# Column tiles, 32-row scores, zero products and turns of heads in an attention-plus-SSM kernel

## The chip, the cores and the metric

The kernel runs on one core of a Trainium2 chip. The metric is the device time of the core in microseconds (us), the median of several executions. The engines are TensorE (PE in the profile; PEld is its weight loads), VectorE (DVE), ScalarE (ACT), GpSimd (POOL) and SyncE (SP). ns is nanoseconds.

## The reference

Two independent halves are joined along the last axis. Half A is a complex diagonal state-space model (SSM), half B attention with 32 query heads of 20 columns and one key/value head, both over 2048 positions of 640 columns in bf16.

```python
def _A_ref(x, ...):                       # cut
    Bu = jnp.einsum("bld,pd->blp", x + 0j, B_bar)
    for t in range(L):
        h = Lam_bar[None, :] * h + Bu[:, t, :]
    # ... stacked to hseq
    y = 2.0 * jnp.einsum("blp,dp->bld", hseq, Cmat).real + x * Dskip
def _B_ref(x, wq, wk, wv, wo):            # S=2048, D=640, H=32, Dh=20
    scores = jnp.einsum("bhqd,bkd->bhqk", q, k) * (Dh ** -0.5)
    p = _softmax(scores, axis=-1)
    o = jnp.einsum("bhqk,bkd->bhqd", p, v)
    # ... heads joined, @ wo
```

## The kernel before

The work is cut into 2048 score tiles of 128 keys by 512 queries, in 32 blocks of four heads. Each tile needs one score product, an exponential, and one or more products with V (PV below) that add into one PSUM bank per block.

- A score product uses 21 rows of the array (20 head columns and a bound that keeps the exponential in range). Four heads lie at partitions 0, 32, 64 and 96, so up to four score products run side by side in row tiles (four start at 302.92 us in the timeline below).
- The exponential of most tiles is done by ScalarE, in groups of three and two tiles (tiles SC to PR). The others go to VectorE (tiles MB to DR), which builds the bits of four shifted bf16 values; their sum is the exponential. Such a tile costs four VectorE instructions and four PV products.
- A PV product has 32 output columns, so four heads run side by side in column tiles (four start within 10 ns at 302.37 us below).
- Everything else (projections, the SSM, the normalization, the output products) is "background", on the whole 128x128 array.

The static order on every engine comes from a planner in the kernel itself: it steps through a model of the engines, in which each operation has a duration, and picks the ready operation of the best priority.

```python
class Schedule:
    OUT = {"pe": 200.0, "act": 130.0, "dve": 110.0, "pool": 150.0, "dma": 60.0}
    OWN = {"pe": 0.0, "act": 60.0, "dve": 55.0, "pool": 100.0}
    # ... no cost for a change of the array's shape
class Build:
    CHUNKS = (3, 2)   # score tiles per ScalarE instruction
    MISC = 2          # PSUM banks shared by background and VectorE's tiles
    NPS = 5
    NDS = 4
    SHARE = 0.215
    # ...
    def mm(self, out, lhsT, rhs, start, stop, **kw):
        return lambda e: e.matmul(out, lhsT=lhsT, rhs=rhs, start=start, stop=stop, **kw)
    def score(self, op, m, out, bank):
        # ...
        op.fns.append(self.mm(out, p.KT[32 * j:32 * j + 21, 128 * kc:128 * kc + 128],
                              p.QT[32 * j:32 * j + 21, qb % 2, gg, :], True, True, tile_position=(32 * j, 0)))
    def pv(self, op, b, group):
        # ...
            op.fns.append(self.mm(bank.tensor[32 * j:32 * j + 32, bank.off:bank.off + 512], lhs, rhs,
                                  first, last, tile_position=(0, 32 * j), skip_group_check=True))
```

Of the kernel before, what the change touches and what calls it, by code (L numbers as in the profile page):

```python
# [20 lines left out]
class Op:  # L21
# [3 lines left out]
                 "seq", "land", "dma_key", "idx", "tail")  # L25

    def __init__(self, eng, fns, dur, deps=(), prio=5, reads=(), writes=(), prev=None, gate=None, hook=None,
                 dma_key=None, land=0.0, tail=0.0):
        self.eng, self.fns, self.dur = eng, list(fns), dur
        self.deps, self.prio, self.prev = list(deps), prio, prev  # L30
        self.reads, self.writes = list(reads), list(writes)
        self.gate, self.hook = gate, hook
        self.dma_key, self.land, self.tail = dma_key, land, tail
        self.start = self.end = None
        self.seq = self.idx = 0


class Schedule:
# [7 lines left out]
    OWN = {"pe": 0.0, "act": 60.0, "dve": 55.0, "pool": 100.0}  # L46
    URGENT = 1.0

    def __init__(self):
        self.t = 0.0  # L50
        self.pending = {e: [] for e in self.ENGINES}
        self.free = {e: 0.0 for e in self.ENGINES}
        self.order = []
        self.events = []
        self.procs = []
        self.dma_free = {}
        self.n = 0
        self.sources = {e: [] for e in self.ENGINES}
        self.slack = {"pe": 60.0, "dve": 150.0}

# [40 lines left out]
    def begin(self, op, eng):  # L101
        if op.hook is not None:
            op.hook(op)
        op.start = self.t
        if op.dma_key is not None:
# [9 lines left out]
        for lag in (0.0, 55.0, 60.0, 100.0, 110.0, 130.0, 150.0, 200.0):  # L115
            self.at(op.end + lag)

    def pick(self, eng):
        best = None
# [3 lines left out]
        for src in self.sources[eng]:  # L123
            extra = src()
            if extra is not None:
                cands = cands + [extra]
        for op in cands:
# [5 lines left out]
            if r <= t + 1e-6:  # L133
                if best is None or (op.prio, op.seq) < (best.prio, best.seq):
                    best = op
            elif op.prio <= self.URGENT and (urgent is None or r < urgent):
                urgent = r
        if best is None:
            return None
        if urgent is not None and best.prio > self.URGENT and t + best.dur > urgent + self.slack.get(eng, 1e9):  # L140
            return None
# [203 lines left out]
class Build:  # L345
    CHUNKS = (3, 2)
    MISC = 2
    NPS = 5
    NDS = 4
    SHARE = 0.215  # L350

    SHIFTS = ((0, 0.24037683), (32, 0.20213201), (64, 0.16997209), (96, 0.14292892))

# [49 lines left out]
    def alloc(self, o):  # L403
# [9 lines left out]
        self.QT = sb(o, "QT", [128, 2, NGG, 512], BF16)  # L413
# [3 lines left out]
        self.DR = sb(o, "DR", [128, self.NDS, len(self.SHIFTS), 512], I16)  # L417
        self.WO4 = sb(o, "WO4", [128, NGG, 640], BF16)
        self.PR = sb(o, "PR", [128, self.NPS, 3, 512], BF16)
# [13 lines left out]
        self.lift = sb(o, "lift", [128, 2], FP32)  # L433
# [20 lines left out]
    def alloc_late(self, s):  # L454
        self.W = self.sb(s, "W", [128, NC, 2, 512], BF16)
        self.g = self.sb(s, "g", [128, 2, 2, 512], BF16)
        self.OT = self.sb(s, "OT", [128, 12, 512], BF16)
        self.LATE = [f"W{c}" for c in range(NC)] + [f"g{u}_{i}" for u in range(2) for i in range(2)] \
            + [f"OT{i}" for i in range(12)]


    def pe(self, fns, dur, **kw):
        return self.s.add("pe", fns, dur, **kw)
# [28 lines left out]

    def mm(self, out, lhsT, rhs, start, stop, **kw):
        return lambda e: e.matmul(out, lhsT=lhsT, rhs=rhs, start=start, stop=stop, **kw)  # L494

    @staticmethod
    def mmt(n, k=1):
        return n / 2.3 * 1.0 + 8.0 * k
# [10 lines left out]
    def program(self):  # L509
# [5 lines left out]
        self.evac_op, self.norm_op = {}, {}  # L515
# [7 lines left out]
        self.d_per = {}  # L523
# [16 lines left out]
        self.s.sources["pe"].append(self.d_source)  # L540

    def warm_source(self):

        if self.started or self.s.t > 40000.0:
# [3 lines left out]
                  deps=[self.zero_op], reads=["PR0"], writes=[self.pvbank.key], hook=self.warm_last)  # L548
# [4 lines left out]
    def constants(self):  # L553
# [19 lines left out]
        many("VP", [lambda e: e.memset(p.VP[:], 0.0), lambda e: e.memset(p.VP[:, :, 20:21], 1.0)], 500)  # L573
# [3 lines left out]
        for k, (_, c) in enumerate(self.SHIFTS):  # L577
            fns.append(lambda e, k=k: e.memset(p.VS[:, k, :, 20:21], hi[k]))
            fns.append(lambda e, k=k, c=c: e.memset(p.VS[:, k, :, 21:22], c - hi[k]))
        many("VS", fns, 250)  # L580
        many("maskM", [
# [22 lines left out]
                                               channel_multiplier=1)], 250)  # L604
        rows = self.dve(lambda e: e.tensor_reduce(out=p.lift[:, 0:1], in_=p.E1[:], axis=AX.X, op=ALU.add), 120,
# [147 lines left out]
    def qt_task(self, qb, gg, bank):  # L753
        p = self
        prev = None
        slot = qb % 2
        for c in range(NC):
# [3 lines left out]
                           prio=3, reads=[f"xbT{qb}", "wq4"], writes=[bank.key])  # L761
        dst = p.QT[:, slot, gg, :]
        key = f"QT{slot}_{gg}"
# [11 lines left out]
        if qb == 0 and gg == 0:  # L775
            for c in range(NC):
# [7 lines left out]
                          deps=[m, self.lift_op], reads=[bank.key, "lift"], writes=[key, "QTr0_0"], prio=0.4)  # L784
# [14 lines left out]
    def row_task(self, qb, half, bank):  # L799
        p = self  # L800
        slot = qb % 2
# [3 lines left out]
        fns = [self.mm(bank.tensor[0:32, bank.off:bank.off + 512], p.Mm[:, gg, :], p.aq[:, gg % 4, :], gg == ggs[0],  # L805
                       gg == ggs[-1]) for gg in ggs]
        prev = self.pe(fns, 4 * self.mmt(512), deps=[self.mm_op] + [self.qt_op[(qb, gg)][1] for gg in ggs] + bank.last,
                       prio=1.5, reads=["Mm"] + [f"aq{i}" for i in range(4)], writes=[bank.key])
# [4 lines left out]
        if qb == 0 and half == 0:  # L813
            lo, ng = 1, 3
        fns = [lambda e, j=j: e.dma_start(p.QT[32 * j + 20:32 * j + 21, slot, lo:lo + ng, :],
# [3 lines left out]
                                           reads=[f"brow{rs}"] + [f"QT{slot}_{gg}" for gg in range(lo, lo + ng)],  # L819
                                           writes=[f"QTr{slot}_{gg}" for gg in range(lo, lo + ng)], prio=0, land=500.0)  # L820
# [13 lines left out]
    def attention(self):  # L834
# [10 lines left out]
        while self.tile_n < NTILE:  # L845
# [14 lines left out]
            fill = self.pe([], self.mmt(512, 2), deps=deps, prio=0, hook=lambda op, i=i: self.fill(op, i))  # L860
            self.next_fill = fill
            k += 1

    def fill(self, op, i):
# [7 lines left out]
        extra = None  # L872
        if self.want_d():
            tiles.append(self.tile_n)
            self.tile_n += 1
            extra = min(tiles, key=lambda m: self.d_per.get((m // 64, m % 4), 0))
            tiles.remove(extra)
# [4 lines left out]
        if extra is not None:  # L882
            self.fill_d(op, extra)
        op.reads = sorted(set(op.reads))
        op.dur = self.mmt(512, len(op.fns))
        dst = p.PR[:, h.index, 0:n, :]
        ex = self.act(lambda e: e.activation(dst, t[:, 0:512 * n], ACT.Exp, scale=1.0 / UNIT), 0.833 * 512 * n + 93,  # L887
# [12 lines left out]
    def score(self, op, m, out, bank):  # L900
# [5 lines left out]
        op.fns.append(self.mm(out, p.KT[32 * j:32 * j + 21, 128 * kc:128 * kc + 128],  # L906
                              p.QT[32 * j:32 * j + 21, qb % 2, gg, :], True, True, tile_position=(32 * j, 0)))
        op.reads += [f"KT{kc // 4}", f"QT{qb % 2}_{gg}", f"QTr{qb % 2}_{gg}"]
# [3 lines left out]
    def want_d(self):  # L912
        s = self.s
        if self.tile_n >= NTILE - 8 or self.d_count + 1 > self.SHARE * (self.tile_n - 16):
            return False
        if self.d_bank() is None:
            return False
        h = self.dhold[self.ndhold % self.NDS]
        return not h.taken or (h.left == 0 and s.done(h.users))

    def d_source(self):

        f = self.next_fill
        if f is None or f.start is None and f.deps and self.d_count == 0:
            return None
        if f.start is None:
            r = self.s.ready(f)
            if r is not None and r < self.s.t + self.ALONE:
                return None
        b = self.tile_n // 64  # L930
        if not self.started or not self.want_d() or not self.block_ready(b):
# [5 lines left out]
        def hook(op):  # L937
            self.tile_n += 1
            self.fill_d(op, self.tile_n - 1)
            op.reads = sorted(set(op.reads))  # L940
        return Op("pe", [], self.mmt(512, 1), prio=0.95, hook=hook)

    next_fill = None
    ALONE = 450.0

    def d_bank(self):
        s = self.s
        for b in self.free_banks:
            if all(o.end is not None and s.seen(o, "pe") <= s.t for o in b.last):
                return b  # L950
        return None
# [6 lines left out]
    def fill_d(self, op, m):  # L958

        p = self  # L960
        bank = self.d_bank()
# [4 lines left out]
        self.d_per[(m // 64, m % 4)] = self.d_per.get((m // 64, m % 4), 0) + 1  # L966
# [4 lines left out]
        first = self.dve(self.ts(p.DR[:, h.index, 0, :], bank.ap, 16256.0, 0.0, ALU.add, ALU.max), 600, deps=[op],  # L971
                         reads=[bank.key], writes=[k0], prio=0.5)
        self.s.spawn(self.d_give(bank, first))
        for k, (sh, _) in enumerate(self.SHIFTS):
            key = f"DR{h.index}_{k}"
            o = first
            if k:
                o = self.dve(self.ts(p.DR[:, h.index, k, :], p.DR[:, h.index, 0, :], float(sh), None, ALU.add), 200,
                             deps=[first], reads=[k0], writes=[key], prio=0.55)
# [3 lines left out]
    def pv_source(self):  # L983
# [23 lines left out]
        prio = 0.9 if tight else 2.0  # L1007
        return Op("pe", [], self.mmt(512, len(group)), prio=prio, hook=lambda op: self.pv(op, b, group))
# [5 lines left out]
    def pv(self, op, b, group):  # L1014
        p = self
        bank = self.pvbank
        for j, e in group:
            lhs, kc, rhs, key, ex, h, vk = e
# [20 lines left out]
    def norm_task(self, b, bank):  # L1039
# [3 lines left out]
        ot = b % 12  # L1043
        m1 = self.pe([self.mm(bank.cols(4 * i, 4 * i + 4), src[:, 128 * i:128 * i + 128], p.E1[:], True, True)
                      for i in range(4)], 4 * 65, deps=[self.evac_op[b], self.c_op["E1"]] + bank.last, prio=1.6,
                     reads=[f"pvsb{slot}", "E1"], writes=[bank.key])

        def rc(e):
            with p.nc.allow_low_precision("bf16 reciprocal of softmax denominator"):
                return e.reciprocal(p.rdT[:, slot, :], bank.cols(0, 16))  # L1050
        r = self.dve(rc, 230, deps=[m1], reads=[bank.key], writes=[f"rdT{slot}"], prio=1.2)
        spread = bass.AP(tensor=p.rdT, offset=16 * slot, ap=[[32, 128], [1, 16], [0, 32]])
        x = self.pool(lambda e: e.tensor_copy(p.rdX[:, slot, :, :], spread), 700, deps=[r], reads=[f"rdT{slot}"],  # L1053
                      writes=[f"rdX{slot}"], prio=1)
        fns = [self.mm(bank.cols(128 * i, 128 * i + 128),
                       p.rdX[:, slot, 4 * i:4 * i + 4, :].rearrange("p j d -> p (j d)"), p.ident[:], True, True)
               for i in range(4)]
        m2 = self.pe(fns, 4 * 65, deps=[x, self.c_op["ident"]], prio=1.6, reads=[f"rdX{slot}", "ident"],
                     writes=[bank.key])
        d = self.dve(self.tt(p.OT[:, ot, :], src, bank.ap, ALU.mult), 630, deps=[m2],  # L1060
# [406 lines left out]
```

## Time and profile before

985.23 us median of 3 runs (984.86 to 987.18); the profiled execution took 980.32. Lines of the page of before: busy us and share of each engine; busy tenths in 40 slices of the span; PEclk, the granted TensorE clock in tenths; and the shares of the chain of waits that ended last.

```profile
PE 908.5 (93%) x6555; PEld 262.0 (27%) x6555; DVE 741.0 (76%) x1899; ACT 813.4 (83%) x699; POOL 32.2 (3%) x66
...
ACT  3597789988777999977979999899798979688992
...
PEclk8987679966557999976969999799697868689987
...
PE 65%; DVE 19%; ACT 11%; issue 3%; DMA 1%; ACTq 0%; POOL 0%; POOLq 0%; DVEq 0%
...
L494 PE MATMUL SC<-QT,KT 21*128 21x512 bf16 x1711 | 303.7, 439 | 36.7 <-ACT PR L887 20.9
L506 DVE TENSOR_SCALAR DR<-MB 128x512 int16<-128x512 f32 x337 | 230.8, 687 | 121.7 <-PE MB L494 110.7
```

TensorE is the busiest engine and has most of the chain. ScalarE, which has the exponentials, has holes all along. The last two lines give the split: 1711 score tiles go to ScalarE and 337 to VectorE.

A busy share of TensorE can deceive, as matmuls overlap (below, each takes 0.39 to 0.61 us while the next group starts 0.32 to 0.54 us after it). The start times are surer. Timeline of TensorE in before, two short stretches (start us, us, engine, line, what, shapes, count):

```profile
302.37 0.61 PE L494 MATMUL MB<-DR,VS 128*32 128x512 bf16 x1
302.38 0.61 PE L494 MATMUL MB<-PR,VP 128*32 128x512 bf16 x1
302.38 0.61 PE L494 MATMUL MB<-DR,VS 128*32 128x512 bf16 x2
302.92 0.60 PE L494 MATMUL MB<-QT,KT 21*128 21x512 bf16 x1
302.92 0.61 PE L494 MATMUL SC<-QT,KT 21*128 21x512 bf16 x3
...
308.35 0.39 PE L494 MATMUL SC<-QT,KT 21*128 21x512 bf16 x2
308.67 0.39 PE L494 MATMUL MB<-PR,VP 128*32 128x512 bf16 x1
308.67 0.39 PE L494 MATMUL MB<-DR,VS 128*32 128x512 bf16 x1
308.68 0.39 PE L494 MATMUL MB<-PR,VP 128*32 128x512 bf16 x2
309.00 0.60 PE L494 MATMUL MB<-xbT,wq 128*128 128x512 bf16 x2
```

Four PV products start within 10 ns and count as one group. In the second stretch a group starts 0.32 to 0.33 us after one of another shape, and two of the same shape can start 0.216 us apart. In the first stretch the same step takes 0.54 us; there the clock's record stands at 0.5 (until 307.4 us, then at 1.0). Over all 512-column groups after 45 us, with the clock records laid beside them: same shape (PV after PV, whole array after whole array) at least 215 ns, median 225 to 226, at full clock, and at least 398, median 401 to 405, at half; change of shape, medians of 312 to 332 and 535 to 567. By these figures a change cost about 100 ns at full clock (312 less 215 is 97) and about 140 at half.

In the record of before the clock is either 1.0 or 0.5, in steps of 3.4 us (its periods are multiples of 3.413 us). After the start (from about 41 us on, to the end of the clock's record) it stands at half for 318 us in 24 periods, one of them 61 us long.

### The profile page before, as it was taken

Reading aid. Unit: us, or ns where it says so; the run is one execution under the profiler, and the core shown is the slowest. Engines: PE = TensorE matmul, PEld = TensorE weight load, DVE = VectorE, ACT = ScalarE, POOL = GpSimd, SP = SyncE. Lnnn points to the kernel's source line nnn. Section 1 sums busy time; section 2 is a strip of 40 time slices with the busy share of each in tenths; the row PEclk is TensorE's granted clock in tenths of the full one; section 3 lists DMA queues with packets and bytes.
Section 4 is the critical chain, followed back from the end, with each engine's and each line's share of the span. In section 5 each row is a group of like instructions: output and inputs, shape, how many; then the busy total and the mean of one; then the engine's idle time right before and its main releaser. Section 6 shows DMA issues by size and latency. Waiting matters only on the chain.

```text
span 978.6 us, 16125 instructions
## 1 busy us (share of the span) xinstructions
PE 908.5 (93%) x6555; PEld 262.0 (27%) x6555; DVE 741.0 (76%) x1899; ACT 813.4 (83%) x699; POOL 32.2 (3%) x66
## 2 busy tenths in 40 slices
PE   7889999999899999999899999989999999998997
PEld 2322222222123322222233322222332322223323
DVE  6987678978775588876956797799576868688672
ACT  3597789988777999977979999899798979688992
POOL 4000000000000000000000000000000000000000
PEclk8987679966557999976969999799697868689987
DMA  9740000000000010000000100000000000000000
GB/s 164 118 87 1 1 2 1 1 1 2 2 1 6 23 38 12 7 1 1 2 6 17 34 11 8 11 1 1 5 14 12 1 11 6 6 6 1 17 12 27
DMA packets 49147, 16.63 MB, mean 17 GB/s; under 512 B 43572, under 2 KB 49072, under 8 KB 49072
## 3 DMA queue, kind: packets, MB, share of 16 engines
q1 hardware_dynamic: 44480, 14.72, 7.1%
q10 hardware_dynamic: 4592, 0.88, 0.7%
q8 instruction: 52, 0.85, 0.4%
q14 instruction: 23, 0.19, 0.1%
HBM read 1.69 MB, written 5.24 MB: 7 GB/s over the span
## 4 chain that ended last, share of the span: by engine, by line
PE 65%; DVE 19%; ACT 11%; issue 3%; DMA 1%; ACTq 0%; POOL 0%; POOLq 0%; DVEq 0%
PE MB L494 47%; PE SC L494 18%; ACT PR L887 11%; DVE DR L506 7%; DVE DR L505 6%; DVE prod L501 1%; DMA vec<-in_A_Dskip_dram 1%; DVE pvsb L1032 1%; DVE stg L1098 1%; DVE u L501 0%; DVE g L1255 0%; DVE W L501 0%; DVE fr L506 0%; DVE QT L769 0%; ACTq L485 0%
## 5 line engine op out<-in xcount | busy, mean ns | idle before, releaser
L887 ACT ACTIVATE PR<-SC 128x1536 bf16<-128x1536 f32 (+1 forms) x685 | 802.2, 1244 | 124.9 <-PE SC L494 71.8
L494 PE MATMUL MB<-PR,VP 128*32 128x512 bf16 x1711 | 339.5, 448 | 4.4 <-DVE pvsb L1032 1.9
L494 PE MATMUL SC<-QT,KT 21*128 21x512 bf16 x1711 | 303.7, 439 | 36.7 <-ACT PR L887 20.9
L506 DVE TENSOR_SCALAR DR<-MB 128x512 int16<-128x512 f32 x337 | 230.8, 687 | 121.7 <-PE MB L494 110.7
L494 PE MATMUL MB<-DR,VS 128*32 128x512 bf16 x1348 | 311.2, 465 | 1.9 <-DVE pvsb L1032 1.6
L505 DVE TENSOR_SCALAR DR<-DR 128x512 int16<-128x512 int16 x1011 | 233.5, 288 | 9.8
L494 PE MATMUL MB<-QT,KT 21*128 21x512 bf16 x337 | 147.6, 439 | 7.3 <-DVE DR L506 4.4
L494 PEld LDWEIGHTS SC<-QT,KT 21*128 21x128 bf16 x1711 | 67.3, 93 | 291.8 <-issue 132.1
L494 PEld LDWEIGHTS MB<-PR,VP 128*32 128x32 bf16 x1711 | 73.0, 97 | 120.5 <-issue 95.6
L494 PEld LDWEIGHTS MB<-DR,VS 128*32 128x32 bf16 x1348 | 66.2, 100 | 74.3 <-issue 55.7
L494 PE MATMUL MB<-xaT,BT 128*128 128x512 bf16 x200 | 73.2, 440 | 1.6 <-DVE DR L506 1.6
L494 PE MATMUL MB<-CT,W 128*128 128x128 bf16 (+1 forms) x320 | 63.0, 313 | 0.0
L494 PE MATMUL MB<-xbT,wq 128*128 128x512 bf16 x165 | 54.8, 424 | 1.3 <-DVE QT L769 1.1
L494 PE MATMUL MB<-WO,OT 128*128 128x128 bf16 (+1 forms) x256 | 53.1, 346 | 0.7 <-DVE DR L506 0.5
L501 DVE TENSOR_TENSOR prod<-MB,Z 128x1024 bf16<-128x1024 f32 x40 | 48.4, 1211 | 6.5 <-PE MB L494 6.4
L1053 POOL COPY rdX<-rdT 128x512 bf16<-128x512 bf16 x32 | 22.3, 698 | 916.7 <-DVE rdT L1050 916.7
L1098 DVE CAST stg<-MB 128x512 bf16<-128x512 f32 x40 | 27.4, 684 | 30.9 <-PE MB L494 30.8
L494 PEld LDWEIGHTS MB<-QT,KT 21*128 21x128 bf16 x337 | 31.2, 93 | 49.3 <-DVE DR L506 20.5
L1255 DVE TENSOR_TENSOR_SCAN g<-sc,hst,u 128x512 bf16<-128x512 f32 x30 | 38.2, 1285 | 0.0
L501 DVE TENSOR_TENSOR OT<-pvsb,MB 128x512 bf16<-128x512 bf16 x32 | 21.8, 682 | 19.4 <-PE MB L494 19.3
L1032 DVE CAST pvsb<-MB 128x512 bf16<-128x512 f32 x32 | 21.9, 685 | 17.7 <-PE MB L494 17.4
L494 PEld LDWEIGHTS MB<-CT,W 128*128 128x128 bf16 x320 | 22.9, 101 | 27.7 <-issue 22.5
(100 smaller groups left out, 335.4 us busy)
## 6 DMA issues: line engine op xcount, KB each, us to landing
out_dram<-stg SPq DMA_DIRECT2D x40, 128.0 KB, 1.7
wqr<-in_B_wq_dram ACTq DMA_DIRECT2D x1, 800.0 KB, 9.9
WO<-in_B_wo_dram SPq DMA_DIRECT2D x4, 200.0 KB
QT<-brow SPq DMA_DIRECT2D x28, 4.0 KB
xaT<-in_A_x_dram SPq DMA_TRANSPOSE x15, 2.7
xbT<-in_B_x_dram SPq DMA_TRANSPOSE x10, 4.7
BT<-in_A_B_re_dram SPq DMA_TRANSPOSE x5, 3.5
BT<-in_A_B_im_dram SPq DMA_TRANSPOSE x5, 3.0
```

The costliest lines, as they stand in the source:

```text
L494: return lambda e: e.matmul(out, lhsT=lhsT, rhs=rhs, start=start, stop=stop, **kw)
L501: return lambda e: e.tensor_tensor(out, a, b, op)
L505: return lambda e: e.tensor_scalar(out, a, s1, None, op0=op0)
L506: return lambda e: e.tensor_scalar(out, a, s1, s2, op0=op0, op1=op1)
L887: ex = self.act(lambda e: e.activation(dst, t[:, 0:512 * n], ACT.Exp, scale=1.0 / UNIT), 0.833 * 512 * n + 93, deps=[op], reads=[b.key for ...
L1032: ev = self.dve(lambda e: e.tensor_copy(p.pvsb[:, slot, :], bank.ap), 620, deps=[op], reads=[bank.key], writes=[f"pvsb{slot}"], prio=0.6, ...
L1053: x = self.pool(lambda e: e.tensor_copy(p.rdX[:, slot, :, :], spread), 700, deps=[r], reads=[f"rdT{slot}"], writes=[f"rdX{slot}"], prio=1)
L1098: ev = self.dve(lambda e: e.tensor_copy(st, bank.ap), 620, deps=[prev], reads=[bank.key], writes=[key], prio=1.8, gate=(lambda: last.end i ...
L1255: o = self.dve(lambda e, ri=ri, init=init: e.tensor_tensor_scan(p.g[:, u, ri, :], rdec, p.u[:, ri, :], init, ALU.mult, ALU.add), 1280, dep ...
```

## The change

Its parts, with their intent:

1. Background products run as four 32-column tiles, so they have the shape of PV and a change of shape is saved.
2. Scores read 32 rows, 11 of them zeros in both operands, to use more of the array.
3. Where the last 3 us of the plan used little of the array, four zero products are added to the open PV bank.
4. Tiles for VectorE are taken from the four heads in turn, so that PV groups are full more often, and more of them may go into one group of scores. The target share goes from 0.215 to 0.25.
5. The planner learns the cost of a change of shape (97 ns) and better durations; there are more PR buffers (7 in place of 5) but fewer for QT (12 in place of 16) and OT (10 in place of 12), the normalization has two steps, and priorities change.

```diff
+    SWITCH, STAY = 97.0, 1.2
     ...
+            if op.mode != self.mode:
+                op.dur += self.SWITCH
+                self.mode = op.mode
+            self.loads.append((self.t, op.load))
     ...
-    NPS = 5
+    NPS = 7
-    SHARE = 0.215
+    SHARE = 0.25
     ...
     def mm(self, out, lhsT, rhs, start, stop, **kw):
+        if self.quads() and lhsT.shape[-1] == 128 and not kw:
+            def four(e):
+                for j in range(4):
+                    r = e.matmul(out[32 * j:32 * j + 32], lhsT=lhsT[:, 32 * j:32 * j + 32], rhs=rhs, start=start,
+                                 stop=stop, tile_position=(0, 32 * j), skip_group_check=True)
+                return r
+            return four
     ...
+    KEEP = 3200.0
+    def keep_source(self):
+        ... # none while the bank is closed
+        if self.s.recent(3000.0) > self.KEEP:
+            return None
+        fns = [self.mm(bank.tensor[32 * j:32 * j + 32, bank.off:bank.off + 256], p.VZ[:], p.xbT[:, 0, 0:256], False,
+                       False, tile_position=(0, 32 * j), skip_group_check=True) for j in range(4)]
     ...
-        op.fns.append(self.mm(out, p.KT[32 * j:32 * j + 21, 128 * kc:128 * kc + 128],
-                              p.QT[32 * j:32 * j + 21, qb % 2, gg, :], True, True, tile_position=(32 * j, 0)))
+        op.fns.append(self.mm(out, p.KT[32 * j:32 * j + 32, 128 * kc:128 * kc + 128],
+                              p.QT[32 * j:32 * j + 32, b % 12, :], True, True, tile_position=(32 * j, 0)))
     ...
-            extra = min(tiles, key=lambda m: self.d_per.get((m // 64, m % 4), 0))
+            extra.append(min(tiles, key=self.d_weight))
```

The rest (buffer indices, priorities, the split of the normalization) is cut.

## The prediction

> **What bounds it now.** TensorE. The page gives PE 93%, ACT 83%, DVE 76%; the chain of waits is PE 65%, DVE 19%, ACT 11%. From the timeline of PE I took start-to-start times of groups of products after the 45 us start-up. Groups come in three shapes: scores in row tiles (21x128), PV in column tiles (128x32), the rest whole-array (128x128). At full clock a 512-column group takes 216 ns when the next has the same shape and 310-320 ns when it differs: a change of shape costs about 100 ns [...]. Medians sit on these minima, so PE is truly full. There are about 690 entries into scores, each two changes, and about 270 changes between column and whole-array products.

> Clock: mean granted 0.833, only 1.0 or 0.5 in 3.4 us steps, so a third of the time is at half clock (100 to 300 us: 0.80, 0.59). At 0.5 the same steps take 398 and 535 ns. Summed over the groups, half clock costs about 125 us, shape changes about 160 us, other waits 60-90 us. The clock falls only in windows where little of the array was used: my estimate from the trace is under about 0.4 of the cells, scores counted as 32 rows. [...]

> **What the change does.**
> 1. Whole-array products become four concurrent 32-column products, one shape with PV: about 270 changes go, -25 us. 512-column ones should stay at 216 ns per four (PV does that now). 128-column ones (about 500, 56 ns now) may become issue-bound near 100 ns (the 4-column products start 25 ns apart now): +20 us. About 4,500 more products.
> 2. [...] clock 0.83 to about 0.97. Worth 100-110 us of PE.
> 3. VectorE's share: 337 tiles now, target 0.25 (508); I expect 400-460. Each moved tile saves ScalarE about 0.45 us (1458+1032 ns per five tiles, partly overlapped), costs VectorE about 1.3-1.38 us (0.69 + 0.69 union) and PE three more PV products (0.16 us). ScalarE -40 us, VectorE +100 to +140, PE +15. Taking turns fills PV groups: now 388 of 942 are not full; some 30 us back on PE.
> 4. Deeper buffers, a schedule that knows the shape change: fewer waits, perhaps -30 us.

> **On the path.** PE would fall from about 930 to about 770 us of work after start-up. Then VectorE (277 us of other work + 1.3 x 420 = about 825) and ScalarE (1630 tiles x 0.447 + 55 = about 785) bind. So not all the PE saving is seen: VectorE becomes the limit, at 93-96% busy.

> **Prediction: 868 us, range 825 to 930.** Faster by over 2%: 0.88; within 2%: 0.07; slower by over 2%: 0.05.

> **What would show it.**
> - Granted clock over 0.95 with hardly any slice under 0.9: step 2. If 0.85-0.9, the zeros don't hold it.
> - Start-to-start of column groups 216 ns across former whole-array products; 128-column fours at 56 or 100 ns: step 1.
> - Count of VectorE tiles 400-460, VectorE busy over 90%, ScalarE 85-90%, idle ScalarE under 80 us: step 3.
> - Chain of waits: PE share down from 65%, DVE up from 19%.

> **What would make it wrong.** TensorE's sequencer can't feed about 11,000 products with as many weight loads, and small fours cost over 150 ns: then 920-960. VectorE takes the full 508 tiles and becomes the bound at 277 + 1.3 x 508 = 940. The plan's idle slots aren't the chip's, so the clock still drops: 900-930. Or VectorE overlaps better (about 1.2 us a tile) and all engines fill: 820.

Step 2 is about the 32 rows and the zero products together. The "0.4 of the cells" is an estimate from the trace of before, from the rows, columns and length of each product in each 3.4-us step: counted so, the highest step just before one of its 24 falls comes to 0.41 with scores as 32 rows, and to 0.36 with the 21 that are read.

## The result, and the profile after

846.74 us median of 4 runs (845.73 to 848.84), against 985.05 (982.81 to 987.18) for before; ratio 0.8599, 95% interval 0.8572 to 0.8626. A ratio here is the mean time of one kernel's fast runs over that of the other's in the same rounds, so not quite the ratio of the medians. The page of the changed kernel, same lines:

```profile
PE 755.4 (90%) x10995; PEld 249.2 (30%) x10995; DVE 710.3 (84%) x1831; ACT 794.3 (94%) x705; POOL 33.6 (4%) x67
...
ACT  2699999999989999999999999998999999999992
...
PEclk8998999999989999999899999999999999998999
...
ACT 83%; PE 9%; DVE 3%; issue 2%; DMA 1%; SPq 1%; POOLq 0%; POOL 0%
...
L532 PE MATMUL SC<-QT,KT 32*128 32x512 bf16 x1728 | 274.1, 391 | 66.9 <-ACT PR L955 51.0
L547 DVE TENSOR_SCALAR DR<-MB 128x512 int16<-128x512 f32 x320 | 217.8, 687 | 65.0 <-PE MB L532 62.1
...
L532 PE MATMUL MB<-xbT,VZ 128*32 128x256 bf16 x736 | 36.3, 278 | 0.0
```

The bound has moved from TensorE to ScalarE, with 83% of the chain. The granted clock rose from 0.833 to 0.971; the time at half clock fell from 318 us to 44 us, in 8 periods of at most 6.8 us (one of them just before the end). VectorE's tiles went from 337 down to 320, so ScalarE has slightly more to do than before, but hardly waits. The last line is the zero products: 184 fours.

How full ScalarE is can be worked out. Three- and two-tile exponentials take turns. In both traces the next starts no sooner than 1330 ns after the start of a three-tile one, and no sooner than 903 or 904 ns after that of a two-tile one. Before: 342 of each, 765 us, in the 925 us between its first and last: 160 us lost. After: 346 and 345, 772 us, in 794 us: 22 us lost. The rest of the 844 us span is 33 us before the first and 16 us after the last exponential.

Timeline of TensorE after:

```profile
500.60 0.39 PE L532 MATMUL SC<-QT,KT 32*128 32x512 bf16 x3
500.61 0.39 PE L532 MATMUL MB<-QT,KT 32*128 32x512 bf16 x1
500.92 0.40 PE L528 MATMUL MB<-WO,OT 128*32 128x512 bf16 x4
501.15 0.38 PE L532 MATMUL MB<-PR,VP 128*32 128x512 bf16 x2
501.16 0.38 PE L532 MATMUL MB<-DR,VS 128*32 128x512 bf16 x1
501.16 0.38 PE L532 MATMUL MB<-PR,VP 128*32 128x512 bf16 x1
501.47 0.39 PE L532 MATMUL SC<-QT,KT 32*128 32x512 bf16 x2
```

The four tiles of an output product (MB<-WO,OT, at 500.92) pass into PV in 0.23 us, with no change of shape; scores to and from the others still cost 0.31 to 0.32.

### The profile page after: what moved, and what is told of

Read it like the earlier page. It is cut to its first block, busy times and chain, and to the rows that moved or that the text cites. A ratio compares the mean times of both kernels' runs of the same rounds, so it can differ in the third digit from the quotient of the medians.

```text
span 843.9 us, 25038 instructions
## 1 busy us (share of the span) xinstructions
PE 755.4 (90%) x10995; PEld 249.2 (30%) x10995; DVE 710.3 (84%) x1831; ACT 794.3 (94%) x705; POOL 33.6 (4%) x67
## 4 chain that ended last, share of the span: by engine, by line
ACT 83%; PE 9%; DVE 3%; issue 2%; DMA 1%; SPq 1%; POOLq 0%; POOL 0%
ACT PR L955 83%; PE MB L532 4%; PE SC L532 3%; PE MB L528 3%; DVE DR L547 1%; DMA xbT<-in_B_x_dram 1%; SPq L517 1%; DVE pvsb L1100 0%; DVE VS L546 0%; DVE OT L542 0%; DVE u L542 0%; DVE QT L547 0%; DVE W L542 0%; DVE sc L1203 0%; DVE stg L1175 0%
## 5 line engine op out<-in xcount | busy, mean ns | idle before, releaser
L532 PE MATMUL SC<-QT,KT 32*128 32x512 bf16 x1728 | 274.1, 391 | 66.9 <-ACT PR L955 51.0
L532 PE MATMUL MB<-PR,VP 128*32 128x512 bf16 x1728 | 262.3, 394 | 4.7 <-DVE pvsb L1100 3.2
L532 PE MATMUL MB<-DR,VS 128*32 128x512 bf16 x1280 | 238.3, 397 | 2.9 <-DVE pvsb L1100 1.7
L532 PEld LDWEIGHTS SC<-QT,KT 32*128 32x128 bf16 x1728 | 69.2, 91 | 326.4 <-ACT PR L955 251.0
L532 PE MATMUL MB<-QT,KT 32*128 32x512 bf16 x320 | 121.7, 390 | 0.7 <-DVE DR L547 0.2
L528 PE MATMUL MB<-CT,W 128*32 128x128 bf16 (+1 forms) x1280 | 63.8, 300 | 0.0
L528 PE MATMUL MB<-xaT,BT 128*32 128x512 bf16 x800 | 63.7, 387 | 0.0
L528 PE MATMUL MB<-WO,OT 128*32 128x512 bf16 (+1 forms) x1024 | 48.3, 308 | 0.1
L528 PE MATMUL MB<-xbT,wq 128*32 128x512 bf16 x560 | 44.6, 382 | 1.6 <-DVE QT L835 1.1
L532 PE MATMUL MB<-xbT,VZ 128*32 128x256 bf16 x736 | 36.3, 278 | 0.0
```

What stands on the lines that cost most here:

```text
L528: r = e.matmul(out[32 * j:32 * j + 32], lhsT=lhsT[:, 32 * j:32 * j + 32], rhs=rhs, start=start, stop=stop, tile_position=(0, 32 * j), skip ...
```

## The experiments

I state two theories. CLOCK: the gain is mostly the granted clock, and zero products, 32 rows and four tiles hold it. ORDER, its rival: the gain is mostly the new order (parts 4 and 5: fuller groups, a better-informed plan, buffers), and the clock follows from that. "The plan" in the expectations is the planner's own reckoning, no measurement. Where an experiment says "very order", only what the products do was changed and the planner was not told, so the order of instructions is that of its parent.

All results in one table. Ratios are to before in the same rounds. Half clock and ScalarE loss are from each profiled run, worked out as above; ScalarE loss is the time between its first and last exponential beyond the back-to-back time. An execution counts as slow here when it is over 1.5% above the fastest of its kernel: the medians are of all executions, the ratios of the fast ones. Profiles marked * fell in a slow run. The executions of e6 spread from 934 to 958 us, two of four slow; e2, e3 and e9 have one slow one each. "Replanned" means that the edit changed the plan a little: e6 and e10 have 335 tiles on VectorE where before has 337, e11 has 312 and e12 294 where the changed kernel has 320.

| run | order | zeros | 32 rows | four tiles | median us | ratio | clock | half clock us | ScalarE loss us |
|---|---|---|---|---|---|---|---|---|---|
| before | old | no | no | no | 985.1 | 1 | 0.833 | 318 | 160 |
| e8_before_rows32 | old | no | yes | no | 909.4 | 0.924 | 0.938 | 100 | 85 |
| e6_before_zeros* | old, replanned | yes | no | no | 946.3 | 0.952 | 0.889 | 202 | 133 |
| e9_before_four_tiles | old | no | no | yes | 950.7 | 0.962 | 0.865 | 241 | 118 |
| e10_before_all | old, replanned | yes | yes | yes | 878.8 | 0.893 | 0.967 | 46 | 60 |
| e5_order_only | new | no | no | no | 926.0 | 0.942 | 0.834 | 299 | 97 |
| e3_zeros_off_rows21 | new | no | no | yes | 902.0 | 0.919 | 0.847 | 272 | 79 |
| e1_zeros_off | new | no | yes | yes | 868.6 | 0.884 | 0.929 | 112 | 38 |
| e2_rows21 | new | yes | no | yes | 867.8 | 0.881 | 0.929 | 111 | 40 |
| e4_full_array* | new | yes | yes | no | 852.8 | 0.866 | see below | 38 | 39 |
| e13_changed_again | new | yes | yes | yes | 846.0 | 0.864 | 0.973 | 44 | 22 |
| e11_more_zeros | new, replanned | more | yes | yes | 847.7 | 0.865 | 0.972 | 42 | 19 |
| e12_no_turns | new, replanned | yes | yes | yes | 855.6 | 0.870 | 0.988 | 12 | 20 |

All gave correct results.

### New order without the three parts, old order with them

```diff
# e5, against the changed kernel
-        self.n_keep += 1
+        self.n_keep += 1; fns = []            # zero products planned, none emitted
-        if self.quads() and lhsT.shape[-1] == 128 and not kw:
+        if False:                              # whole-array products
# ... and 32 * j + 32 back to 32 * j + 21 in the score product
```

> The new order of instructions, buffers and priorities kept exactly as in the changed kernel, but whole-array products again, 21 rows in the scores, and no zero products. Theory CLOCK (the gain is mostly the granted clock, and the zero products, 32 rows and four tiles hold it): falls back to 930 us or more, clock 0.86 or less. Theory ORDER (the gain is mostly the new order: fuller groups, fewer changes of shape, a plan that knows what they cost; the clock follows from that): 900 us or less, clock 0.90 or more.

Measured 925.98 us, clock 0.834: between the two forecasts, and with no gain at all in the clock. The new order alone is worth 5.8%, at the same 0.83 clock as before. ORDER's second half, that the clock follows from the order, falls here. Page of e5 (clock and chain):

```profile
PEclk8966997985569999889579999995999957857987
...
PE 46%; ACT 42%; DVE 8%; issue 3%; DMA 1%; SPq 1%; POOLq 0%; POOL 0%
```

e10 is the old kernel with `mm` as in the change, the 32 rows, and `keep_source` with its count of recent use carried over; its planner still knows no cost for a change of shape.

> The old kernel and its old planner, with the three hardware parts put in: zero products by the same rule, 32 rows, four column tiles. Theory CLOCK: 895 us or less, clock 0.94 or more. Theory ORDER: 930 us or more; the clock may rise, but the stale plan (840 us planned, 980 us run) still leaves ScalarE idle for over 100 us.

Measured 878.76 us, clock 0.967: 10.7% from the three parts alone. Page of e10:

```profile
PEclk8889999999999999999799999999999999999899
...
PE 46%; DVE 35%; ACT 13%; issue 4%; SPq 1%; DMA 1%; POOL 1%; POOLq 0%; DVEq 0%
```

So CLOCK carries the larger part. The two don't multiply: 0.893 x 0.942 is 0.841, and together they gave 0.860. I read this as both saving part of the same waiting, which was not tested. What the order adds on top of e10 is ScalarE loss, 60 to 22 us, at the same half-clock time (46 and 44 us). Which part of the order does that (buffers, costs in the plan, priorities) was not separated; only the turns of heads were, in e12.

### Each part taken out of the changed kernel

```diff
# e1
-        self.n_keep += 1
+        self.n_keep += 1; fns = []
# e2
-        op.fns.append(self.mm(out, p.KT[32 * j:32 * j + 32, 128 * kc:128 * kc + 128],
-                              p.QT[32 * j:32 * j + 32, b % 12, :], True, True, tile_position=(32 * j, 0)))
+        op.fns.append(self.mm(out, p.KT[32 * j:32 * j + 21, 128 * kc:128 * kc + 128],
+                              p.QT[32 * j:32 * j + 21, b % 12, :], True, True, tile_position=(32 * j, 0)))
# e3: both.  e4:
-        if self.quads() and lhsT.shape[-1] == 128 and not kw:
+        if False:
```

The windows "of the array used" in these expectations are my estimates from the trace of the changed kernel, by the method under e8, with the zeros or the 11 rows left out of the count.

> The changed kernel in its very order, only the zero products are not emitted. CLOCK: the falls of the clock double (from 8 to about 16; my count of 3.4 us windows with under 0.36 of the array used goes from 13 to 26), clock about 0.93 or less and 865 us or more. ORDER: clock stays over 0.95, under 855 us.

868.61 us, clock 0.929, 20 falls in place of 7 (not counting the one at the very end): as CLOCK expected. These 184 fours of products that add zero save 22 us.

Two theories go with the rows. ROWS: the granted clock follows the number of rows that the scores read. NO ROWS: it doesn't. (In the expectation of e2 the second forecast is that of NO ROWS.)

> The changed kernel in its very order, 21 rows in the scores in place of 32; the products give the same numbers. [...] the windows of 3.4 us with under 0.36 of the array used go from 13 to 22 by my count: some 12 to 15 falls, clock 0.94 to 0.95, +8 to +15 us. [...] (theory NO ROWS): no change, 847 us, clock 0.97.

867.79 us, clock 0.929. Eleven rows of zeros in each score product save about 20 us (22 by the medians, 18 by the means of the fast runs, as two of the six took 857), somewhat more than the 8 to 15 I expected, and change no instruction's count or place. NO ROWS falls.

> The changed kernel in its very order, 21 rows and no zero products, the four tiles kept. Without zeros alone it took 869 us (clock 0.929), without all three parts 926 us (0.834). ROWS: the rows carry most of those 57 us: 900 to 920 us, clock 0.87 or less (windows under 0.36: 45 in place of 26). NO ROWS: stays near 869 us, and then the four column tiles carry the 57 us where no zeros fill the gaps.

902.01 us, clock 0.847: ROWS again. 56 us above the control (54 by the fast runs), more than the two singly sum to: with both gone the clock stays down longer (periods of 11.2 us on average, against 5.5 without zeros and 9.1 without rows).

> The changed kernel in its very order, only the background products run on the whole array again. 306 more changes of shape by my count in the trace, at 97 ns each 30 us of TensorE. CLOCK and ORDER both: if TensorE still bound the kernel, +30 us (875 us); as ScalarE binds now (94% busy), only part shows, 855 to 870 us. If the four tiles cost as much in issue as they save, 847 us.

852.76 us. The ratio, 0.8664 (0.8612 to 0.8715), overlaps that of the changed kernel (0.8599; on another chip 0.8637), so in the new order the four tiles are worth 0.3 to 0.8%, and this is not clear of the noise. Some 300 changes of shape came back (1606 in e4 against 1310, from 45 us on), by my estimate at 97 ns each (312 less 215, above) about 30 us of TensorE, and 6 us of it show; I take the rest to have gone into its slack, which was not tested. Without zeros and 32 rows the same step is larger: e5 against e3, which differ in the four tiles alone, is 0.942 against 0.919 (on two chips). And e5 against e4, on one chip, gives zeros and rows together without the four tiles: 926 to 853 us.

The profiled run of e4 was slow for a reason of its own: its clock records show 0.85 where the other profiled runs show 1.0 (mean 0.833, against 0.968 to 0.972 in its fast runs). So only its fast runs count here (851.1 to 854.3 us, clock 0.968 to 0.972). A window of the slow one (stretch in us and its length; busy us and instructions of PE, PEld, DVE, ACT, POOL; granted clock; DMA share; GB/s):

```profile
300.00:400.00 100.00, 95.92 (x783) 27.74 (x781) 87.67 (x203) 99.51 (x88) 2.59 (x4) 0.85 0.03 9
```

### Each part alone in the kernel before

The edits are the reverse of those above, in the old kernel.

> The old kernel in its very order, only 32 rows in the scores (11 of them zeros). In the new order the rows were worth 22 us with zero products and 33 without. ROWS: 950 to 965 us, clock 0.86 to 0.89. If the rows matter only together with the new order: 982 us.

909.35 us: 7.6% from two numbers in one line, in the very order of before. It is the largest single part, over half of the whole gain, and I had expected 20 to 35 us, not 75. Page of e8:

```profile
PE 806.8 (89%) x6472; PEld 255.2 (28%) x6555; DVE 736.7 (81%) x1899; ACT 805.5 (89%) x699; POOL 32.1 (4%) x66
...
PEclk8898999998589999999679999999997999999987
```

PEclk is now mostly 9 where before had runs of 5 to 7, and TensorE is busy 102 us less for the same products (83 of 6555 records are missing from this trace, which explains only a small part). At a given clock the products took the same with 21 rows and with 32 (from scores to PV the median is 321 ns at full clock and 539 at half, with either), so of what I compared the granted clock alone is left to explain it. The sizes agree: 218 us less at half clock, at 216 in place of about 400 ns for the same group, is by estimate 100 us of TensorE.

> The old kernel and planner with the zero products alone (21 rows, whole-array background). The old plan is 140 us too short, so its idle slots are not the chip's. If they must fall into the chip's true gaps to work: 970 us or more. If any added activity helps: 940 to 960 us, clock 0.87 to 0.90.

946.32 us; the two fast runs took 933.76 and 939.63 at clock 0.91. Before took 983.64 in the same rounds, at 0.82 to 0.83: the zero products helped, though the plan's idle slots are not the chip's.

> The old kernel in its very order, only the four column tiles. 273 changes of shape go, at about 100 ns: 27 us at full clock, some more at half: 945 to 958 us if TensorE binds throughout. If the four tiles cost as much as they save (issue of four times as many products): 975 us or more. All three parts together gave 879 us.

950.68 us, as expected for a bound TensorE. But half-clock time fell too, from 318 to 241 us, so this 3.8% mixes the saved changes of shape with a gain in clock, and the runs don't separate them.

The three singly give 7.6, 4.8 and 3.8%, 16.2% if summed; together 10.7%. They compete for the same half-clock time: singly they take 218, 116 and 77 us off it, 411 in all, and before has 318.

### More zeros, and no turns

```diff
# e11
-    KEEP = 3200.0
+    KEEP = 4000.0
# e12, in d_weight
-        return self.d_per[m // 64, m % 4], m
+        return 0, m
```

e13 is the changed kernel, run beside e2, e3 and e11 on one chip.

> The changed kernel once more, as the control of this group of runs on one chip: 847 us, clock 0.97.

> The changed kernel planned with its threshold for zero products at 4000 in place of 3200, so about twice as many are planned. If the zeros cost time (they take TensorE's slots), +5 us or more. If the left falls of the clock can be filled: clock 0.98 or more and 835 to 842 us. My view: the left falls come where the PV bank is closed and no zero product can be issued, so the clock stays at 0.97 to 0.98 and the time at 843 to 850 us.

845.96 us and 847.67 us, clock 0.973 and 0.972: no difference. More zero products (1452 in place of 736) cost nothing that shows and don't lift the clock further, though the plan changed a little with them (8 more tiles on ScalarE, 3 us more of its work). The fall of the clock at 235.8 us, which I followed in the trace of the changed kernel, comes at the end of a block: from 231.5 to 236.5 us TensorE runs only four groups of scores while VectorE finishes its tiles, and the planner puts no zero product into a PV bank that is about to close. That this is why more zeros don't help is argued from the trace, not tested. This was my try at a version better than the changed kernel; it isn't one. Four microseconds of that stretch, with columns as for e4 above:

```profile
232.00:236.00 4.00, 1.57 (x12) 0.42 (x12) 3.86 (x13) 4.00 (x5) 0.00 (x0) 0.98 0.00 0
```

> The changed kernel without the turns of heads: the tile for VectorE is always the first of the group. The plan changes with it: 294 tiles on VectorE in place of 320, and less full PV groups. 26 tiles more on ScalarE at 0.447 us is 12 us, so 857 to 865 us if ScalarE binds; 847 us if the turns don't matter.

855.64 us, 0.7 to 1.1% above the changed kernel by the ratios (0.8697 against 0.8637 and 0.8599, each on another chip; the intervals of the first two overlap). Here 294 tiles go to VectorE, ScalarE's back-to-back time rises to 784 us from 772, and its loss stays at 20 us: the difference is those 12 us. Counted in the planner, PV groups of fewer than four products go from 87 (of 792) to 377 (of 907). And the clock is the best of all:

```profile
PEclk8899999999999999999999999999999999999999
```

A clock of 0.988 with 855.64 us, against 0.971 with 846.74 for the changed kernel: with ScalarE at 86% of e12's chain, the clock was no longer the measure.

## Why the prediction was right, and where it was wrong

The total was 868 (825 to 930), measured 846.7, faster by over 2% as held most likely. That the total came so near is in part luck: the limit that was named, VectorE with about 825 us of work, did not form (710 us busy), and the one that did, ScalarE, happens to lie at a similar height. Point by point:

- **TensorE bound before, with about 125 us of half clock and 160 us of changes of shape in its 930:** right in kind. e8 shows the clock's part in the cleanest way: the instructions and their order are the same, half-clock time falls and the kernel is 7.6% faster. The medians do not quite "sit on the minima": they are 10 ns above (226 and 216).
- **Step 1, four tiles, -25 us and +20 us:** the first is near what e9 shows in the old order (3.8%, part of it clock) and far over what e4 shows in the new one (0.3 to 0.8%). The +20 us didn't come. At full clock fours of 128 columns start 56 ns apart, the same as one whole-array product in before, and fours of 4 columns 25 ns apart (25 to 26 in before). TensorE took 10,995 products and as many weight loads, and neither step got longer.
- **Step 2, clock 0.83 to about 0.97, worth 100 to 110 us:** right in the clock, 0.971 measured. The worth was forecast as TensorE's time, which no run shows by itself. In the kernel's time, zeros and rows give 73 us in the new order without the four tiles (e5 to e4) and 56 with them (e3 to e13); all three parts in the old order gave 10.7%, about 105 us, of which some belongs to the saved changes of shape. I didn't say which part does it; the rows alone do 7.6%, the zeros alone 4.8%.
- **Step 3, "I expect 400-460" tiles on VectorE, "VectorE becomes the limit":** wrong, and the step that failed. The count fell to 320 and ScalarE became the limit. I read the share of 0.25 as the setting that decides. It isn't binding: 337 of 2048 tiles is 0.165, well under even the old target, and the changed kernel built with the share back at 0.215 is the same program, instruction for instruction, on every engine. So the other conditions decide. Built once more with each refusal counted, the planner turns VectorE down at 449 of its 691 groups of scores: at 365 for want of a free PSUM bank, at 74 for a buffer, at 10 for the share or the end of the tiles (all within the first or last 20). That is the plan's own count; no run with more banks was made. The total came out 21 us too high because I had VectorE at 825 us of work, binding at 93 to 96%. In its place stands ScalarE with 772 us back to back, 22 us lost and 49 us of start and end, 843 in all. The signs named for this step missed with it: VectorE is busy 84% (over 90% forecast) and its share of the chain fell from 19% to 3% (a rise was forecast); ScalarE is busy 94% (85 to 90%). My own formula for ScalarE (0.447 us a tile and 55) gives 827 us for the 1728 tiles that it got, so had the tile count been right, it would have shown ScalarE as the next limit.
- **Taking turns fills PV groups:** right. By the planner's count 359 of 916 PV groups were not full before, 87 of 792 after, 377 of 907 without turns (my 388 of 942, counted in the trace, had split some groups). The forecast "30 us back on PE" does not show as such: the turns are worth 0.7 to 1.1%, and that by way of ScalarE's load.
- **Step 4, fewer waits, -30 us:** right in size. e10 to the changed kernel is the new order with all parts present: 0.893 to 0.860, about 32 us. That has the turns in it, so the buffers and the plan alone may be nearer 20 (an estimate, 32 less the 9 to 12 of e12). "Deeper buffers" holds for PR alone.

## What to carry to other kernels

Look at the granted clock before counting products: here a TensorE that was busy 93% with narrow products was given half the clock for a third of the time (318 of 979 us), and padding the contraction from 21 rows to 32 with zeros that are already in memory was worth more than a reorganization (7.6% against 5.8%). Zero products in idle slots were worth 4.8% in the old order and 22 us in the new one. Such gains can overlap (16.2% summed, 10.7% together) and stop at the next engine; here ScalarE's back-to-back time (772 us) was the wall, and near it (e12) 12 us more of its load made the kernel longer at a higher clock. A tuning constant is a lever only if it binds: check what a build does with the old value before costing the new one.
